# K-transposed-V and query products of an attention and experts kernel, from block-diagonal full-array matmuls to 64-wide tiles

## The chip, the cores and the metric

The kernel runs on one core of a Trainium2 chip. It is one program; its time is the device time from the first to the last instruction in microseconds. A core has engines with queues of their own: TensorE (PE: matmuls, PEld: weight loads), VectorE (DVE), ScalarE (ACT), GpSimd (POOL) and SyncE (SP, which issues most loads here). TensorE reads from SBUF and writes to PSUM, which has 8 banks of 128 partitions by 512 fp32 values.

## The reference

Linear attention without softmax, a norm per head, a layer that takes the maximum of three products, and a layer of eight experts with two experts a token:

```python
kv  = einsum('bhsd,bhse->bhde', k, v)        # 8 batches, 8 heads, 576 tokens, 64 wide
out = einsum('bhsd,bhde->bhse', q, kv)
x   = out / sqrt(mean(out*out, -1) + 1e-6) * g_norm      # then 4608 tokens x 512
h   = maximum(maximum(x @ w1, x @ w2), x @ w3)            # 512 -> 768
x   = h @ w_out                                           # 768 -> 512
logits = x @ w_gate;  noisy = logits + log1p(exp(x @ w_noise)) * noise
# each token: its two best experts e, softmax weight w_e of the two noisy logits
out[token] += w_e * (maximum(x @ e_w1[e], 0) @ e_w2[e])   # 512 -> 1024 -> 512
```

## The kernel before

The 4608 tokens go in 9 chunks of 512, each of four token tiles of 128. The batches of 576 tokens do not line up with the chunks. After the last chunk come the experts, in units of up to 512 tokens; that is the part from about 650 us to the end, and the change does not touch it.

A chunk c has 18 groups of the maximum layer (`g1`, matmuls on line 308), each 12 matmuls: three fp32r passes over the four quarters of the 512 inputs. Its output product (`g2`, line 353) follows in the function `window`, one token tile after the other. Between these stands the attention for the next chunk, written into fixed places of that order by hand:

- in `misc1`, group 10: the K-transposed-V product of batch c + 1 (`kv_pair`, line 188), and `kv_out`, which copies it to SBUF;
- in group 14: the query product (`ao`, lines 209 and 212) of the next chunk's token tiles 0 and 1, and their norms;
- in `window`, between the second and the third token tile: transposes of tiles 0 and 1 (`xtrans`, line 270), the query product of tiles 2 and 3, and their norms; in the middle of the fourth tile's output product the transposes of tiles 2 and 3.

K-transposed-V has one matmul for each pair of heads p (four) and each piece s of 128 tokens (five, the last half filled with zeros). A matmul contracts 128 tokens and gives 128 by 128 values, of which the two 64 by 64 blocks on the diagonal are the two heads. `kv_out` copies these blocks into a buffer KB (`kvbd`) whose other blocks were set to zero at the start. The query product then takes, for each pair of heads, the transposed queries (128 rows: two heads of 64) as weights and KB's 128 by 128 block as the streamed operand. Where a token tile holds tokens of two batches, its halves of 64 tokens are done apart, with 64 weight columns each (line 212). All operands of these two products are fp32; a matmul of them shows in the trace as two weight loads and two matmul records.

A norm (`norm`) is a square on ACT (line 229), a sum per head on DVE (233), a few small steps and the scaling on DVE (249). `xtrans_pe` turns 128 by 128 blocks with TensorE, ACT and DVE then write the high part (line 274) and the low part (279) of x.

Banks come from two rings of four: HB (`hbank`) for the maximum layer, transposes and late query products, AC (`abank`) for the output product, K-transposed-V and early query products. In the start-up (chunk 0 and half of chunk 1) a small planner, `run_tasks`, orders the instructions of all engines by costs and dependences given for each task (`kvp`, `ao`, `n1s`, `t0` and so on); weights arrive as 64-bit numbers there (w1s) and are converted and split by ACT and DVE.

## Time and profile before

| what | value |
|---|---|
| runs | 1589.89 us median of 3 (1589.64 to 1590.69) |
| profiled execution, first to last instruction | 1588.9 us |
| mean granted TensorE clock | 0.997 |
| PE busy | 1564.8 us, 98% of the span |
| DVE, ACT busy | 740.6 us (47%), 608.0 us (38%) |
| chain that ended last | PE 96% |

The profiled execution is shown by its span alone; its time as a run, outside the profile, is not among the three runs of the table. "Busy" sums the times in which an engine had an instruction under way; matmuls overlap, so that the distance between the starts of two stretches says more than a busy time. In a timeline several instructions of one form are merged into a row with their count (xcount); such a row's second number is the time from its first start to its last end, which runs past the next row's start.

### The profile page before, as it was taken

How to read it: one execution, taken by the hardware profiler on the slowest of the kernel's cores; microseconds unless marked ns; L12 is line 12 of the kernel's file. 1: busy time of each engine (PE TensorE's matmuls, PEld its weight loads, DVE VectorE, ACT ScalarE, POOL GpSimd, SP SyncE). 2: the span in 40 equal slices, each digit the busy share in tenths (PEclk: the TensorE clock that was granted, in tenths of full speed). 3: DMA queues.
4: the chain of work that ended last, by engine and by line, in shares of the span. 5: the costliest groups of instructions: out<-in, count | busy, mean ns of one | idle time of the engine just before them, and what ended most of it. 6: DMA issues, size and time to landing. Idle time of an engine off the chain costs nothing.

```text
span 1588.9 us, 21936 instructions
## 1 busy us (share of the span) xinstructions
PE 1564.8 (98%) x8716; PEld 1362.3 (86%) x8716; DVE 740.6 (47%) x1416; ACT 608.0 (38%) x981; POOL 221.6 (14%) x326
## 2 busy tenths in 40 slices
PE   6999999999999999999999999999999999999997
PEld 6899989898989898888888888888888888888886
DVE  6984434343434333445543455455354444544543
ACT  4553323131313132332343445545444343544433
POOL 0001111102020202023211102102111010210102
PEclk9999999999999999999999999999999999999999
DMA  8312732031212101132655567557475554746544
GB/s 305 126 70 106 276 144 113 28 113 47 94 54 87 53 28 54 53 134 107 233 153 146 122 216 218 156 189 205 136 207 154 163 160 155 221 121 203 146 153 75
DMA packets 52572, 219.43 MB, mean 138 GB/s; under 512 B 6896, under 2 KB 7152, under 8 KB 34928
## 3 DMA queue, kind: packets, MB, share of 16 engines
q1 hardware_dynamic: 32608, 166.50, 29.2%
q0 software_dynamic: 19856, 51.48, 14.3%
q8 instruction: 70, 1.15, 0.3%
q14 instruction: 38, 0.31, 0.1%
HBM read 166.49 MB, written 51.47 MB: 137 GB/s over the span
## 4 chain that ended last, share of the span: by engine, by line
PE 96%; DVE 1%; DMA 1%; ACT 1%; issue 1%; POOL 0%; SPq 0%; POOLq 0%; DVEq 0%
PE bank L308 27%; PE bank L1098 25%; PE bank L1036 25%; PE bank L353 10%; PE bank L188 2%; PE bank L760 2%; PE bank L209 2%; PE bank L1050 1%; PE bank L270 1%; DMA G<-w1s 1%; PE bank L493 0%; DMA kv<-kv 0%; PE bank L212 0%; PE bank L485 0%; POOL out L1072 0%
## 5 line engine op out<-in xcount | busy, mean ns | idle before, releaser
L308 PE MATMUL bank<-B,W 128*128 128x512 f32 (+1 forms) x2160 | 454.4, 370 | 6.6 <-ACT W L474 4.9
L308 PEld LDWEIGHTS bank<-B,W 128*128 128x128 f32 x2160 | 375.9, 189 | 75.1 <-ACT W L474 5.6
L1098 PE MATMUL bank<-W,B 128*128 128x512 f32 x1728 | 421.1, 390 | 0.2 <-issue 0.2
L1098 PEld LDWEIGHTS bank<-W,B 128*128 128x128 f32 x1728 | 320.2, 188 | 63.4
L1036 PE MATMUL bank<-B,W 128*128 128x512 f32 (+1 forms) x1728 | 356.9, 344 | 0.0
L1036 PEld LDWEIGHTS bank<-B,W 128*128 128x128 f32 x1728 | 278.0, 189 | 40.1
L290 DVE TENSOR_TENSOR W<-G,W 128x1024 fp32r<-128x1024 f32 x200 | 242.5, 1224 | 132.1 <-ACT W L289 131.5
L1040 ACT ACTIVATE B<-bank 128x512 fp32r<-128x512 f32 (+1 forms) x176 | 91.3, 520 | 373.5 <-PE bank L1036 360.2
L1041 DVE SCALAR_TENSOR_TENSOR B<-bank,B 128x512 fp32r<-128x512 f32 (+1 forms) x176 | 104.3, 593 | 270.8 <-ACT B L1040 265.1
L289 ACT ACTIVATE W<-G 128x1024 fp32r<-128x1024 f32 x200 | 207.7, 1054 | 46.8 <-PE bank L1098 39.3
L353 PE MATMUL bank<-W,B 128*128 128x256 f32 (+1 forms) x1296 | 164.2, 285 | 0.0
L353 PEld LDWEIGHTS bank<-W,B 128*128 128x128 f32 x1296 | 160.2, 188 | 0.7 <-issue 0.2
L419 POOL DMA_INDIRECT Xg<-RA,si x72 | 71.6, 994 | 546.7 <-issue 294.2
L326 DVE TENSOR_TENSOR hm<-hm,bank 128x512 f32<-128x512 f32 (+1 forms) x106 | 69.5, 656 | 138.0 <-PE bank L308 122.8
L1036 PE MATMUL bank<-xlo,W 128*128 128x512 f32 x384 | 102.8, 389 | 0.0
L1072 POOL DMA_INDIRECT out<-xn,idt x37 | 61.2, 1653 | 281.3 <-ACT xn L1103 274.3
L312 ACT ACTIVATE B<-hm 128x512 fp32r<-128x512 f32 (+1 forms) x53 | 32.2, 607 | 173.2 <-DVE hm L326 167.5
L1036 PEld LDWEIGHTS bank<-xlo,W 128*128 128x128 f32 x384 | 72.1, 188 | 15.3
L1072 POOL DMA_INDIRECT out<-x2T,idt x19 | 30.9, 1628 | 272.1 <-ACT x2T L1103 269.7
L764 ACT ACTIVATE B<-bank 128x512 fp32r<-128x512 f32 x76 | 41.5, 596 | 42.3 <-PE bank L760 37.0
L358 ACT ACTIVATE RA<-bank 128x256 f32<-128x256 f32 x72 | 26.3, 384 | 76.6 <-PE bank L353 71.8
L324 ACT ACTIVATE hm<-bank 128x512 f32<-128x512 f32 (+1 forms) x53 | 30.4, 574 | 59.3 <-PE bank L308 47.0
(191 smaller groups left out, 1032.5 us busy)
## 6 DMA issues: line engine op xcount, KB each, us to landing
G<-mw SPq DMA_DIRECT2D x100, 1024.0 KB, 4.8
RB<-Xg SPq DMA_DIRECT2D x13, 1028.0 KB, 7.1
G<-w1s SPq DMA_DIRECT2D x12, 1024.0 KB, 6.4
out<-pad POOLq DMA_DIRECT2D x1, 9472.0 KB
kv<-kv SPq DMA_DIRECT2D x8, 1024.0 KB
G<-kv SPq DMA_DIRECT2D x8, 1024.0 KB, 16.6
RB<-qT SPq DMA_DIRECT2D x8, 1024.0 KB, 5.5
RA<-Xg SPq DMA_DIRECT2D x8, 514.0 KB
```

The source lines that it names most:

```text
L289: ACT.activation(w[:, 0:1024], src, AF.Copy)
L290: DVE.tensor_tensor(w[:, 1024:2048], src, w[:, 0:1024].bitcast(F), op=OP.subtract)
L308: PE.matmul(bank[:, 0:t1 - t0], w_in(g)[:, a, k, s], x[b][:, k, t0:t1], start=n == 0 and k == 0, stop=n == 2 and k == 3)
L326: DVE.tensor_tensor(hm, hm, bank, op=OP.max)
L353: PE.matmul(x2b[i][z][:, 0:hi - lo], h[:, a, s], w[:, b, lo:hi], start=f == 0 and n == 0, stop=f == 5 and n == 2)
L419: i = POOL.indirect_dma_start(out=Xg, out_offset=bass.IndirectOffsetOnAxis(ap=idx, axis=0), in_=src, in_offset=None)
L764: ACT.activation(x[0][:, :, s], t, AF.Copy)
L1036: PE.matmul(bank[:, 0:n], w[:, a, k, s], x[b][:, k, 0:n], start=z == 0, stop=z == 11)
L1040: ACT.activation(h[:, 0, 0:n], bank[:, 0:n], AF.Relu)
L1041: DVE.scalar_tensor_tensor(h[:, 1, 0:n], bank[:, 0:n], 0.0, h[:, 0, 0:n].bitcast(F), op0=OP.max, op1=OP.subtract)
L1072: d = POOL.indirect_dma_start(out=A["out"], out_offset=bass.IndirectOffsetOnAxis(ap=idt[u % 3][:, i:i + 1], axis=0), in_=y, in_offset=None ...
L1098: PE.matmul(obank[i], h[:, a, s], w[:, b, ff % 2, :], start=ff == 0 and n == 0, stop=ff == 7 and n == 2)
```

## The change

Each head gets matmuls of its own, on tiles of the array that are 64 wide.

- K-transposed-V: for each pair and piece two matmuls (h = 0, 1), each with the 64 columns of one head's K as weights and that head's 64 columns of V streamed. The result of head h stands in partitions 64h to 64h + 63, and a batch takes 256 columns of a bank instead of 512. `kv_out` is one copy by DVE, and KB (`kvt`) is 128 by 256 without zero blocks, so its memsets go.
- Query product: `ao` now does two token tiles at once. For each tile, pair, half x of 64 tokens and head h there is one matmul: rows of head h, output partitions of half x. Each row half h writes a bank of its own. So a bank now holds one head of each pair, for both token tiles; the norms work on banks, and the transposes of a token tile read both banks' results. The rows of the first weights are put in the order that this gives, on the host.
- The planner's tasks: one task for a pair of token tiles, and other costs. Transposes wait for both norms.

```diff
-    KB = [sb1.tile([128, 4, 128], F, name=f"kvbd{i}") for i in range(2)]
+    KB = [sb1.tile([128, 256], F, name=f"kvt{i}") for i in range(2)]
...
-    DVE.memset(KB[0], 0.0)
-    POOL.memset(KB[1], 0.0)
+    HALF = [slice(0, 64), slice(64, 128)]
...
             k, v = r[s // 2][2 * (s % 2):2 * (s % 2) + 2]
         else:
             k, v = r[2]
-        PE.matmul(out, k[:, p * 128:(p + 1) * 128], v[:, p * 128:(p + 1) * 128], start=s == 0, stop=s == 4)
+        for h in range(2):
+            o = p * 128 + h * 64
+            PE.matmul(out[HALF[h], :], k[:, o:o + 64], v[:, o:o + 64], start=s == 0, stop=s == 4)
     def kv_pair(b, p, bank):
         for s in range(5):
-            kv_mm(b, p, s, bank[:, p * 128:(p + 1) * 128])
+            kv_mm(b, p, s, bank[:, p * 64:(p + 1) * 64])
     def kv_out(b, bank):
-        v = bank.rearrange("p (a e) -> p a e", a=4)
+        DVE.tensor_copy(KB[b % 2], bank[:, 0:256])
+
+    ao_bank = {}
+
+    def ao(c, j, banks):
         for h in range(2):
-            s = slice(h * 64, h * 64 + 64)
-            (ACT.copy if h else DVE.tensor_copy)(KB[b % 2][s, :, s], v[s, :, s])
-
-    ao_bank = {}
-
-    def ao(c, i, bank):
-        ao_bank[c, i] = bank
-        t0 = c * CT + i * 128
-        b0, b1 = t0 // S, (t0 + 127) // S
-        for p in range(4):
-            o = bank[:, p * 128:(p + 1) * 128]
-            if b0 == b1:
-                PE.matmul(o, qv(c)[:, p, i * 128:(i + 1) * 128], KB[b0 % 2][:, p, :], start=True, stop=True)
-            else:
-                for h, b in ((0, b0), (1, b1)):
-                    PE.matmul(o[h * 64:h * 64 + 64], qv(c)[:, p, i * 128 + h * 64:i * 128 + h * 64 + 64],
-                              KB[b % 2][:, p, :], start=True, stop=True)
+            ao_bank[c, 2 * j + h] = banks[h]
+        for i in range(2):
+            t0 = (2 * j + i) * 128
+            for p in range(4):
+                o = slice(i * 256 + p * 64, i * 256 + (p + 1) * 64)
+                for x in range(2):
+                    t = t0 + x * 64
+                    kb = KB[(c * CT + t) // S % 2]
+                    for h in range(2):
+                        PE.matmul(banks[h][HALF[x], o], qv(c)[HALF[h], p, t:t + 64],
+                                  kb[HALF[h], p * 64:(p + 1) * 64], start=True, stop=True)
     xn_of = {}
     xn_n = [0]
...
     xA = [B2[:, x * 1024:x * 1024 + 1024].rearrange("p (k t) -> p k t", k=4) for x in range(2)]
     def xtrans_pe(c, i, TR=None):
-        x = xn_of[c, i]
         TR = hbank() if TR is None else TR
         for k in range(4):
-            PE.transpose(TR[:, k * 128:(k + 1) * 128], x[:, k * 128:(k + 1) * 128], ident)
+            x = xn_of[c, 2 * (i // 2) + k // 2]
+            o = (i % 2) * 256 + (k % 2) * 128
+            PE.transpose(TR[:, k * 128:(k + 1) * 128], x[:, o:o + 128], ident)
         return TR
     def xtrans_hi(i, t, xT=xT):
...
-            kv_mm(0, p, s, AC[p][:, 0:128])
+            kv_mm(0, p, s, AC[p][:, 0:64])
...
-        for h in range(2):
-            s = slice(h * 64, h * 64 + 64)
-            (ACT.copy if h else DVE.tensor_copy)(KB[0][s, p, s], AC[p][s, s])
+        (ACT.copy if p % 2 else DVE.tensor_copy)(KB[0][:, p * 64:(p + 1) * 64], AC[p][:, 0:64])
...
-    for i in range(4):
-        ao(0, i, abank())
-        norm_a(0, i)
+    for j in range(2):
+        ao(0, j, [abank(), abank()])
+        for i in range(2):
+            norm_a(0, 2 * j + i)
...
-        task(f"t0{i}", "PE", 0.44, [f"n0c{i}"] + ([f"t0{i - 1}"] if i else []), t0, 0,
+        task(f"t0{i}", "PE", 0.44, [f"n0c{i | 1}"] + ([f"t0{i - 1}"] if i else []), t0, 0,
...
-        task(f"kvp{p}", "PE", 1.15, ["kv1"] + ([f"kvp{p - 1}"] if p else []), lambda p=p: kv1(p), 1,
+        task(f"kvp{p}", "PE", 0.6, ["kv1"] + ([f"kvp{p - 1}"] if p else []), lambda p=p: kv1(p), 1,
...
-        task(f"ao{i}", "PE", 0.92, ["q1", "kvo", "x0l3"] + (["ao0"] if i else []), lambda i=i: ao(1, i, abank()), 0)
-        task(f"n1s{i}", "ACT", 0.6, [f"ao{i}", f"t0{i + 2}"], lambda i=i: norm_sq(1, i, x1[i]), 0.6)
+        if i == 0:
+            task("ao0", "PE", 1.0, ["q1", "kvo", "x0l3"], lambda: ao(1, 0, [abank(), abank()]), 0)
+        task(f"n1s{i}", "ACT", 0.6, ["ao0", "t03"], lambda i=i: norm_sq(1, i, x1[i]), 0.6)
...
-        task(f"x1t{i}", "PE", 0.44, [f"n1c{i}"], t1, 0, on_ring(f"x1l{i}"))
+        task(f"x1t{i}", "PE", 0.44, ["n1c0", "n1c1"], t1, 0, on_ring(f"x1l{i}"))
...
-    for i in (2, 3):
-        task(f"ao{i}", "PE", 0.92, ["rest11", f"ao{i - 1}"], lambda i=i: (ao(1, i, hbank()), norm(1, i, RB[:, i * 512 - 1024:i * 512 - 512])),
-             3.5, on_ring(f"ao{i}"))
+    def ao_late():
+        ao(1, 1, [hbank(), hbank()])
+        for i in range(2):
+            norm(1, 2 + i, RB[:, i * 512:i * 512 + 512])
+    task("ao1", "PE", 1.0, ["rest11", "ao0"], ao_late, 3.5, on_ring("ao1", 2))
...
-            for i in range(2):
-                ao(c + 1, i, abank())
+            ao(c + 1, 0, [abank(), abank()])
...
-            if nx and i < 2:
-                ao(c + 1, i + 2, hbank())
+            if nx:
+                if i == 0:
+                    ao(c + 1, 1, [hbank(), hbank()])
...
-    w = np.stack([moe_w1, moe_w2, moe_w3], 0).reshape(3, 4, 128, 6, 128)
+    w = np.stack([moe_w1, moe_w2, moe_w3], 0).reshape(3, 4, 2, 64, DF).transpose(0, 2, 1, 3, 4).reshape(3, 4, 128, 6, 128)
```

In the places below the names are of SBUF and PSUM buffers (kv, G: staged K and V; kvbd, kvt: K-transposed-V; RB: queries; xn: normed x; W: split weights; hm: the running maximum); a last number of a name tells the allocations apart.

TensorE in chunk 2, group 10, two small matmuls of the routing (on trib and onesb) and then the first pair of heads of batch 3, before:

```order
L405 MATMUL bank0_105<-Cb_129,onesb_104 128x40
L406 LDWEIGHTS trib_103
L406 MATMUL bank0_105<-Mb_128,trib_103 128x32
L188 MATMUL bank4_109<-kv0_92 128x128 x2
L188 MATMUL bank4_109<-G1_83 128x128 x2
L188 MATMUL bank4_109<-G2_84 128x128
```

and with the change:

```order
L406 MATMUL bank0_105<-Cb_127,onesb_104 128x40
L407 LDWEIGHTS trib_103
L407 MATMUL bank0_105<-Mb_126,trib_103 128x32
L190 MATMUL bank4_109<-kv0_92 64x64 x4
L190 MATMUL bank4_109<-G1_83 64x64 x4
L190 MATMUL bank4_109<-G2_84 64x64 x2
```

Each matmul of 128 by 128 has become two of 64 by 64; the order of the pairs and pieces is the same, and nothing is moved past them.

TensorE in `window` of chunk 2, the transposes of token tiles 0 and 1 and the query product of tiles 2 and 3, before:

```order
L353 MATMUL bank6_111<-W11_81,B2_87 128x272
L270 MATMUL bank1_106<-cst_98,xn0_93 128x128 x4
L270 MATMUL bank2_107<-cst_98,xn1_94 128x128 x4
L209 MATMUL bank3_108<-kvbd1_91,RB_89 128x128 x4
L209 MATMUL bank0_105<-kvbd1_91,RB_89 128x128 x4
L353 MATMUL bank7_112<-W9_79,B1_86 128x256
```

and with the change, the first two of the query product's 32 matmuls:

```order
L271 MATMUL bank1_106<-cst_98,xn0_93 128x128 x2
L271 MATMUL bank1_106<-cst_98,xn1_94 128x128 x2
L271 MATMUL bank2_107<-cst_98,xn0_93 128x128 x2
L271 MATMUL bank2_107<-cst_98,xn1_94 128x128 x2
L212 MATMUL bank3_108<-kvt1_91,RB_89 64x64
L212 MATMUL bank0_105<-kvt1_91,RB_89 64x64
```

The two transposes of each result bank now read two normed tiles, and the matmuls of the query product alternate between two banks, one a head.

DVE in the start-up, from the last step of one conversion (ISA, G1) to the low part of the second weight tile (W1), before:

```order
L457 ISA G1_83<-G1_83,RB_89 128x1024x2
L448 TENSOR_SCALAR RB_89<-G2_84 128x1024
L449 SCALAR_TENSOR_TENSOR RB_89<-G2_84,RB_89 128x1024
L470 SCALAR_TENSOR_TENSOR RA_88<-G1_83 128x1024
L326 TENSOR_TENSOR hm0_96<-hm0_96,bank6_111 128x512
L233 TENSOR_REDUCE stat_121<-xn2_95 128x8
L233 TENSOR_REDUCE stat_121<-x2T0_97 128x8
L237 TENSOR_SCALAR stat_121<-stat_121 128x16
L478 TENSOR_TENSOR W1_71<-RA_88,W1_71 128x1024
```

and with the change:

```order
L458 ISA G1_83<-G1_83,RB_89 128x1024x2
L471 SCALAR_TENSOR_TENSOR RA_88<-G1_83 128x1024
L233 TENSOR_REDUCE stat_119<-xn2_95 128x8
L233 TENSOR_REDUCE stat_119<-x2T0_97 128x8
L479 TENSOR_TENSOR W1_71<-RA_88,W1_71 128x1024
L327 TENSOR_TENSOR hm0_96<-hm0_96,bank6_111 128x512
L237 TENSOR_SCALAR stat_119<-stat_119 128x16
L449 TENSOR_SCALAR RB_89<-G2_84 128x1024
L450 SCALAR_TENSOR_TENSOR RB_89<-G2_84,RB_89 128x1024
```

The planner has put the first steps of the third conversion (on G2) and a maximum (hm) behind the low part of the second weight tile.

## Rows read from the trace of the kernel before

**Rows 1.** the page: busy time, chain by engine, largest matmul group

```profile
PE 1564.8 (98%) x8716; PEld 1362.3 (86%) x8716; DVE 740.6 (47%) x1416; ACT 608.0 (38%) x981; POOL 221.6 (14%) x326
...
PE 96%; DVE 1%; DMA 1%; ACT 1%; issue 1%; POOL 0%; SPq 0%; POOLq 0%; DVEq 0%
...
L308 PE MATMUL bank<-B,W 128*128 128x512 f32 (+1 forms) x2160 | 454.4, 370 | 6.6 <-ACT W L474 4.9
```

**Rows 2.** TensorE's timeline in chunk 3: start us, us, line, op, xcount

```profile
298.99 0.69 PE L188 MATMUL bank<-kv 128*128 128x128 f32 x4
299.52 0.83 PE L188 MATMUL bank<-G 128*128 128x128 f32 x6
...
302.87 0.83 PE L188 MATMUL bank<-G 128*128 128x128 f32 x6
303.46 11.18 PE L308 MATMUL bank<-B,W 128*128 128x512 f32 x48
314.47 1.95 PE L209 MATMUL bank<-kvbd,RB 128*128 128x128 f32 x16
316.18 11.14 PE L308 MATMUL bank<-B,W 128*128 128x512 f32 x48
...
336.81 1.95 PE L209 MATMUL bank<-kvbd,RB 128*128 128x128 f32 x16
338.52 6.84 PE L353 MATMUL bank<-W,B 128*128 128x256 f32 x54
345.19 0.60 PE L270 MATMUL bank<-cst,xn 128*128 128x128 f32 x4
```

**Rows 3.** TensorE's timeline in chunk 2, query product of tiles 0 and 1

```profile
237.53 1.06 PE L209 MATMUL bank<-kvbd,RB 128*128 128x128 f32 x8
238.51 1.09 PE L212 MATMUL bank<-kvbd,RB 128*64 128x128 f32 x16
239.54 11.19 PE L308 MATMUL bank<-B,W 128*128 128x512 f32 x48
```

**Rows 4.** short stretches, line L212 alone: records in flight (x), clock, DMA

```profile
238.50:238.55 0.05, 0.04 (x2) 0.04 (x2) 1.00 0.00 0
238.55:238.66 0.11, 0.11 (x2) 0.11 (x4) 1.00 0.00 0
238.66:238.70 0.04, 0.04 (x4) 0.04 (x4) 1.00 0.00 0
238.70:238.77 0.07, 0.07 (x4) 0.07 (x4) 1.00 0.00 0
238.77:238.80 0.03, 0.03 (x6) 0.03 (x4) 1.00 0.00 0
```

**Rows 5.** TensorE's timeline: matmuls of 16 streamed columns, and what follows them

```profile
102.96 1.86 PE L493 MATMUL bank<-wgn,G 128*128 128x16 f32 x16
104.66 3.11 PE L308 MATMUL bank<-B,W 128*128 128x256 f32 x24
```

**Rows 6.** timelines of ACT and DVE in chunk 3: first square, last scaling

```profile
337.90 0.60 ACT L229 ACTIVATE xn<-bank 128x512 f32<-128x512 f32 x1
...
343.42 0.69 DVE L249 TENSOR_TENSOR x2T<-bank,stat 128x512 f32<-128x512 f32 x1
```

**Rows 7.** the timelines of TensorE and DVE at the end of chunk 1

```profile
173.61 8.96 PE L353 MATMUL bank<-W,B 128*128 128x256 f32 x72
...
177.27 0.43 DVE L316 TENSOR_TENSOR B<-hm,B 128x256 fp32r<-128x256 f32 x1 [0.49 <-ACT B L312]
```

**Rows 8.** the chain that ended last: start us, us, what

```profile
5.66 6.44 PE bank L188 x34
...
13.43 8.07 DMA G<-w1s
...
28.06 5.37 PE bank L308 x16
```

**Rows 9.** SP's waits up to 60 us: total us, times, longest us

```profile
SPq L511 <- PE bank L188: 3.8, 1, 3.8
```


## Prediction

> **What bounds the kernel now.** I read the page's chain first, then TensorE's row there, then TensorE's timeline chunk by chunk, last the DVE and ACT timelines around it. The reader is to see in the chain that TensorE holds 96% of it, and in the page's group that the largest matmul line waited 6.6 us in the whole run, 4.9 of that for one ACT line in the start-up [rows 1]. After the start-up, from about 47 us on, TensorE hardly waits, so an edit that gives it fewer or more nanoseconds moves the end by as much; before that, loads, DVE and ACT set the pace. One chunk of the steady part [rows 2] has three stretches that the change rewrites: the K-transposed-V product of the next batch, 40 records from 298.99 to 303.46 us (4.47 us, 112 ns a record), the query product of its first two token tiles, 16 records from 314.47 to 316.18 (1.71 us), and that of the last two, 336.81 to 338.52 (1.71 us). An fp32 matmul leaves two such records, each a weight load and a stream, so 20 matmuls are 40 records.
>
> **The change part by part.** All counts are of records of the steady part and the second half of the start-up.
>
> K-transposed-V: 40 records become 80, each with 64 weight columns and 64 streamed columns on one of two column halves. Six batches (2 to 7) lie where TensorE sets the end; batches 0 and 1 lie in the start-up.
>
> Query product: 16 records for two token tiles become 64, each 64 by 64 on one of four quarters (two row halves by two column halves). There are 18 such pairs of token tiles; two are in chunk 0 in the start-up, 16 count. In 4 of the 16 a token tile holds two batches and runs on column halves already: there 8 full records and 16 half ones took 237.53 to 239.54, 2.01 us [rows 3].
>
> These half records are the nearest rows to the new form, and the sum hangs on them. Each streams 128 columns through a half with 64 weight columns. In [rows 4] two of them begin within the first 0.05 us, none in the next 0.11, two more by 238.70, none in 0.07, two more by 238.80: two records every 0.11 us. So both halves work at once, and each takes some 110 ns for 128 streamed columns, as the full array does (112). Streaming half as many should halve that; weight loading does not hinder it, since 128 weight columns with only 16 streamed ones pace at 1.70 us for 16 records, 106 ns [rows 5], so 64 need about 53. I take 112/2 = 56 ns a record on one tile: 28 ns a record with two tiles at work, 14 with four.
>
> Going into and out of the halves costs something: 2.01 us less 8 records at 107 ns (1.71/16) and 16 at 55 leaves 0.28 us, which I charge to every tiled stretch, and which the four mixed ones pay already.
>
> With r the ns per tiled record, a K-transposed-V stretch becomes 0.28 + 0.080 r, a query stretch 0.28 + 0.064 r. Gains: 6 x (4.47 - 0.28 - 0.080 r) + 12 x (1.71 - 0.28 - 0.064 r) + 4 x (2.01 - 0.28 - 0.064 r) = 49.2 - 1.504 r us. It crosses zero at r = 33. Bounds of r: 14 for the query product if all four tiles overlap; 55, what the half-array records average, if halving the columns saves nothing because records cannot come faster than in the one row that shows them, or 56 if tiles don't overlap. I take 28 for K-transposed-V and 14 for the query product, the measured pace scaled by columns and by tiles: 6 x 1.95 + 12 x 0.53 + 4 x 0.83 = 11.7 + 6.4 + 3.3 = 21.4 us.
>
> The waits that move: a norm now needs a whole pair of token tiles, and the transposes of either tile need both norms. In the last-two stretch the first square began 1.09 us after the product (337.90, when ACT was free from its other work) and the second norm ended at 344.11 (343.42 + 0.69), 1.08 us before the transposes at 345.19 [rows 2, 6]. With a 1.18 us product (0.28 + 0.90) the first square starts some 0.2 later, the norms end at about 344.3, and TensorE reaches the transposes 0.53 earlier, at 344.66: 0.36 us of cover is left, cost nothing; were it gone, each 0.1 us would cost 0.1 us in each of seven chunks. Queued behind these transposes stand the last 18 records of the output product L353, and behind them the next chunk.
> Chunk 1 has no cover: its groups stream 256 columns, DVE runs the norms before the last split, which lies at 177.27 to 177.70, and TensorE wants its result 34 records of 8.96/72 = 0.124 us after 173.61, at 177.8 [rows 7]. DVE would be 0.3 later and TensorE 0.5 earlier: 0.8 us lost, once (0 to 1).
>
> The start-up. SP's second load of K and V waited 3.8 us for TensorE to read the first, the first weights of the maximum layer (w1s) are queued behind it, and their landing at 21.50 starts the chain that ends with the first wide matmul at 28.06 [rows 8, 9]. The first product took 6.44 us there; with smaller records it follows the loads closely, and what SP issues behind it comes up to 2 us earlier, of which the DMA engines, busy already, pass on part. The planner also puts the second weight split earlier on DVE. Against this stands that TensorE idles longer before 28 us. I take 0.5 us gained, between 1.5 lost and 3 gained. The removed ACT copies and memsets of the block-diagonal buffers lie beside TensorE's work: nothing.
>
> Sum: 21.4 - 0.8 + 0.5 = 21.1 us. The profiled execution spans 1588.9 us; the median of the runs, 1589.89, is 1.0 above that, which I leave as it is: 1588.9 + 1.0 - 21.1 = 1568.8, say 1569 us.
>
> **Rivals.**
> Row halves do not overlap, or matmuls start in the order of the program, so that the two records of one tile hold up the next tile: r is 28 in both products, 49.2 - 42.1 = 7.1, less 0.8, plus 0.5: 1583 us. For it: no row of before splits the rows, and on average two tiles cannot be told from strict order by pace alone. Against: in strict order the first record of the run would start alone, and [rows 4] shows two in the first 0.05 us.
> The Trainium skill, "TensorE: Matmul & The Clock Gate", Part 3 on packing small matmuls, has matmuls start and end in strict program order, only weight loads being pulled ahead; by it the time would be this rival's, and [rows 4] speaks against it.
>
> Records cannot be supplied faster: TensorE is given four times as many instructions for the query product, and the densest row of before holds 55 ns a record over 16 records only. If a longer run can do no better than that pace, r = 55, 49.2 - 82.7 = -33.5, less 0.3: about 1624 us, slower. It decides from r = 33 on. The same price falls due if tiles do not overlap at all, the change then not doing what it says. For it: nothing in the trace shows a longer run under 107 ns a record. Against: four records and four weight loads begin within 0.2 us in [rows 4], and no wait for supply shows.
> The Trainium skill, "TensorE: Matmul & The Clock Gate", Part 1 on the clock gate, gives about 62 ns of sequencer work a matmul where the hardware does not decode it; by it r would be 62 and the time about 1634. The 55 ns average of the half records is under that, but over 16 records only.
>
> Supply at a middle pace, r 33 to 50 for the query product alone: 1588 to 1605 us.
>
> The norms lose their cover: 0.36 us short of need in seven chunks would be 2.5 us, 1571; it lies within the forecast's own range.
>
> **How the numbers follow.** Four tiles overlap as forecast: 0.53, 1562 to 1576. Half the overlap: 0.21, 1577 to 1587. Middle pace, or no difference: 0.11. Supply-bound or no overlap: 0.15. The measurement tells about 0.2%, 3.2 us, from no change: faster takes the first two cases and none of the others, 0.74; same 0.07; slower 0.19. The range of 8 in 10 is 1561 to 1602: the low end has the start-up gaining 3 and the entry cost vanishing in part; the high end leaves out the last case alone.
>
> **What would show it.** Query stretches of the new profile at about 1.2 us with four matmul starts inside some 0.06 us, and K-transposed-V at about 2.5 us, confirm the first case; 2.1 us for the query stretch with pairs of starts is the second; 3.8 us is the third. Transposes that wait for a DVE norm in each window show the lost cover, and a gap before the output product near 177 us the 0.8. The first wide matmul before 28 us shows the start-up term. A forecast off by more than the start-up's bounds with these stretches right would mean that something after 47 us that I take as untouched has moved.

## The result, and the profile after

The changed kernel takes 1573.41 us (median of 4 runs, 1572.87 to 1574.52), the kernel before beside it 1589.77 (1589.45 to 1590.69): a ratio of 0.9897, 95% interval 0.9883 to 0.9911. That is 16.4 us gained where 21 were forecast, inside the range, 4 us above the predicted 1569.

The page of the kernel after, to be read against [rows 1]: busy time of TensorE, the chain by engine, the largest matmul group.

```profile
PE 1543.8 (98%) x9868; PEld 1337.2 (85%) x9868; DVE 740.1 (47%) x1413; ACT 604.5 (38%) x972; POOL 221.3 (14%) x325
...
PE 97%; DMA 1%; DVE 1%; ACT 1%; issue 0%; POOL 0%; SPq 0%; POOLq 0%; DVEq 0%
...
L309 PE MATMUL bank<-B,W 128*128 128x512 f32 (+1 forms) x2160 | 455.7, 371 | 6.6 <-ACT W L475 4.2
```

TensorE has 1152 more records (9868 for 8716) and is busy 21 us less. It still holds nearly the whole chain, and the largest group waits the same 6.6 us as before.

TensorE's timeline in chunk 3, to be read against [rows 2]: start us, us, line, xcount.

```profile
295.91 0.45 PE L190 MATMUL bank<-kv 128*64 128x64 f32 x8
...
297.94 0.52 PE L190 MATMUL bank<-G 128*64 128x64 f32 x12
298.39 11.17 PE L309 MATMUL bank<-B,W 128*128 128x512 f32 x48
309.50 1.16 PE L212 MATMUL bank<-kvt,RB 64*64 64x64 f32 x64
310.59 11.18 PE L309 MATMUL bank<-B,W 128*128 128x512 f32 x48
...
331.36 1.16 PE L212 MATMUL bank<-kvt,RB 64*64 64x64 f32 x64
332.45 6.86 PE L354 MATMUL bank<-W,B 128*128 128x256 f32 x54
339.15 0.38 PE L271 MATMUL bank<-cst,xn 128*128 128x128 f32 x2
```

From start to start the 80 records of the K-transposed-V product take 2.48 us (295.91 to 298.39) where 40 took 4.47, and the 64 of a query product 1.09 (309.50 to 310.59, 331.36 to 332.45) where 16 took 1.71.

The records of the first query stretch inside the first 0.15 us, from the view of short windows, line L212 alone (stretch, its length, PE busy, PEld busy, with the records in flight behind x, then the granted clock and the DMA share and rate):

```profile
309.49:309.52 0.03, 0.02 (x4) 0.02 (x4) 1.00 0.00 0
309.52:309.56 0.04, 0.04 (x4) 0.04 (x5) 1.00 0.00 0
...
309.62:309.64 0.03, 0.03 (x8) 0.03 (x12) 1.00 0.00 0
```

Four matmuls are under way at 309.52, none joins them in the next 0.04 us: the four starts lie 6 to 7 ns apart. By the starts in the trace, from the second group on the groups follow each other every 58.5 ns, 14.6 ns a record. All four tiles work at once.

Where does the difference of the two traces grow? The output product (L353 before, L354 after) starts in chunk 0 at 120.97 before and 123.97 after, in the last chunk at 699.89 and 683.60, by these rows of before

```profile
120.97 0.73 PE L353 MATMUL bank<-W,B 128*128 128x256 f32 x4
...
699.89 0.52 PE L353 MATMUL bank<-W,B 128*128 128x256 f32 x3
```

and these of after:

```profile
123.97 0.75 PE L354 MATMUL bank<-W,B 128*128 128x256 f32 x4
...
683.60 0.64 PE L354 MATMUL bank<-W,B 128*128 128x256 f32 x4
```

So the kernel after is 3.0 us late at the end of the start-up, gains 19.3 us from there to the last chunk, and is 16.3 us ahead. A second profile of the kernel before, `before_again` below, has the first of these points at 122.11 and the same 578.92 us from there to the last chunk: the gain of the steady part is firm, the loss of the start-up is 1.9 or 3.0 by the execution that it is held against. (The two profiled spans, 1588.9 and 1571.0, differ by 17.9; the 1.6 between is the delay in the profile of before that the run `before_again` deals with below. It lies in the experts, which begin at 719 us before and 703 after, not near 650.)

The start-up after, where the 3 us are; rows of before are in [rows 8, 9]. First TensorE's timeline:

```profile
20.56 0.48 PE L190 MATMUL bank<-pad,hm 128*64 128x64 f32 x4 [0.73 <-DMA pad<-kvr]
...
22.93 0.67 PE L190 MATMUL bank<-kv 128*64 128x64 f32 x8
...
24.17 1.56 PE L271 MATMUL bank<-cst,xn 128*128 128x128 f32 x10
...
30.59 5.53 PE L309 MATMUL bank<-B,W 128*128 128x512 f32 x16 [4.20 <-ACT W L475]
```

And ACT's there:

```profile
22.64 1.18 ACT L445 ACTIVATE G<-G 128x1024 int32<-128x1024 uint32 x1 [4.11 <-DMA G<-w1s]
25.11 1.84 ACT L275 ACTIVATE B<-bank,gn 128x512 fp32r<-128x512 f32 x3 [1.29 <-PE bank L271]
26.84 1.11 ACT L454 ACTIVATE G<-G 128x1024 f32<-128x1024 f32 x1
```

The same steps in the kernel before (the piece, the transposes, the first weights):

```profile
19.27 0.46 PE L188 MATMUL bank<-pad,hm 128*128 128x128 f32 x2 [0.37 <-DMA pad<-kvr]
...
20.68 1.47 PE L270 MATMUL bank<-cst,xn 128*128 128x128 f32 x12
...
21.52 1.19 ACT L444 ACTIVATE G<-G 128x1024 int32<-128x1024 uint32 x1 [2.95 <-DMA G<-w1s]
```

TensorE waits until 20.56 for the last piece of batch 1's K and V (`pad<-kvr`, used at 19.27 before), runs all four pairs, and reaches the transposes of x only at 24.17 (20.68 before). On ACT the first weights were ready at 22.64 (21.52 before), but its next step on them (L454, 26.84) stands behind three evacuations of those transposes (L275, 25.11). The first wide matmul starts at 30.59 instead of 28.06.

### The profile page after: what moved, and what is told of

Its sections match the earlier page's. It is cut to its first block, busy times and chain, and to the rows that moved or that the text cites. A ratio compares the mean times of both kernels' runs of the same rounds, so it can differ in the third digit from the quotient of the medians.

```text
span 1571.0 us, 24229 instructions
## 1 busy us (share of the span) xinstructions
PE 1543.8 (98%) x9868; PEld 1337.2 (85%) x9868; DVE 740.1 (47%) x1413; ACT 604.5 (38%) x972; POOL 221.3 (14%) x325
## 3 DMA queue, kind: packets, MB, share of 16 engines
q8 instruction: 79, 1.29, 0.3%
## 4 chain that ended last, share of the span: by engine, by line
PE 97%; DMA 1%; DVE 1%; ACT 1%; issue 0%; POOL 0%; SPq 0%; POOLq 0%; DVEq 0%
PE bank L309 28%; PE bank L1102 26%; PE bank L1040 25%; PE bank L354 10%; PE bank L764 2%; PE bank L190 1%; PE bank L212 1%; PE bank L1054 1%; PE bank L271 1%; DMA pad<-kvr 1%; DMA G<-kv 0%; PE bank L494 0%; ACT B L275 0%; PE bank L486 0%; POOL out L1076 0%
## 5 line engine op out<-in xcount | busy, mean ns | idle before, releaser
L1102 PEld LDWEIGHTS bank<-W,B 128*128 128x128 f32 x1728 | 320.2, 188 | 63.4
L354 PE MATMUL bank<-W,B 128*128 128x256 f32 (+1 forms) x1296 | 164.3, 285 | 0.0
L354 PEld LDWEIGHTS bank<-W,B 128*128 128x128 f32 x1296 | 160.1, 188 | 1.1
L1076 POOL DMA_INDIRECT out<-hm,idt x19 | 32.8, 1727 | 145.1 <-ACT hm L1107 141.3
```

The costliest lines, as they stand in the source:

```text
L354: PE.matmul(x2b[i][z][:, 0:hi - lo], h[:, a, s], w[:, b, lo:hi], start=f == 0 and n == 0, stop=f == 5 and n == 2)
L1076: d = POOL.indirect_dma_start(out=A["out"], out_offset=bass.IndirectOffsetOnAxis(ap=idt[u % 3][:, i:i + 1], axis=0), in_=y, in_offset=None ...
L1102: PE.matmul(obank[i], h[:, a, s], w[:, b, ff % 2, :], start=ff == 0 and n == 0, stop=ff == 7 and n == 2)
```

## The experiments

The start-up can be undone without touching the rest, so most runs split it from the steady part. Times are medians; a ratio is against the kernel before on the same chip.

**s_full: the start-up back on the full array.** Batches 0 and 1 and chunks 0 and 1 get the full-array products, block-diagonal buffers KD beside KB, and one norm a token tile; GpSimd copies batch 1's result to KB later.

```diff
+    def kv_tiled(b):
+        return False if b < 2 else True
+    def ao_tiled(c):
+        return False if c < 2 else True
     def kv_mm(b, p, s, out):
+        if not kv_tiled(b):
+            PE.matmul(out, k[:, p * 128:(p + 1) * 128], v[:, p * 128:(p + 1) * 128], start=s == 0, stop=s == 4)
+            return
...
-        task(f"t0{i}", "PE", 0.44, [f"n0c{i | 1}"] + ([f"t0{i - 1}"] if i else []), t0, 0,
+        task(f"t0{i}", "PE", 0.44, [f"n0c{i}"] + ([f"t0{i - 1}"] if i else []), t0, 0,
-        task(f"kvp{p}", "PE", 0.6, ["kv1"] + ...
+        task(f"kvp{p}", "PE", 1.15, ["kv1"] + ...
```

> Start-up as before (batches 0 and 1 and the query products of chunks 0 and 1 as full-array matmuls, planner's tasks as before), small tiles from batch 2 and chunk 2 on. Both theories: the first wide matmul at 28.1 us, the output product of chunk 0 at 121 us instead of 123.97, time about 1570.4 (1573.4 less 3.0). A theory that the start-up's lateness is made up later anyway says 1573. Under theory A the clock reaches its full level near 10.7 us as in the kernel before.

Measured: 1570.05 us (1569.89 to 1570.91), ratio 0.9875 (0.9860 to 0.9890). TensorE's start-up there:

```profile
19.09 0.46 PE L198 MATMUL bank<-pad,hm 128*128 128x128 f32 x2 [0.53 <-DMA pad<-kvr]
...
20.57 1.87 PE L318 MATMUL bank<-cst,xn 128*128 128x128 f32 x12
...
28.43 5.52 PE L356 MATMUL bank<-B,W 128*128 128x512 f32 x16 [3.16 <-ACT W L522]
```

The piece is used at 19.09, the transposes start at 20.57, the first wide matmul at 28.43, chunk 0's output product at 121.46: the start-up is the old one but for half a microsecond, as was expected. From there to the last chunk (681.25) it takes 559.79 us; the kernel after takes 559.63, the one before 578.92. So the loss lies in the start-up alone, and this kernel is the fastest of the study, ahead of the kernel before beyond doubt, and of the changed one by 3 us, with intervals that still touch (0.9883 to 0.9890).

**s_full_kv and s_full_ao: one product at a time.** As s_full, with only the K-transposed-V product of batches 2 to 7, or only the query product of chunks 2 to 8, on tiles.

```diff
 s_full_kv, against s_full:
     def ao_tiled(c):
-        return False if c < 2 else True
+        return False if c < 2 else False
 s_full_ao, against s_full:
     def kv_tiled(b):
-        return False if b < 2 else True
+        return False if b < 2 else False
```

> Start-up on the full array as in the kernel that took 1570.05 us; after it only the K-transposed-V product of batches 2 to 7 is on tiles, every query product is a full-array one. If the two products' gains are separate and add up, the time is 1570.05 + 11 x 0.52 + 3 x 0.85 = 1578.3 us (1577 to 1579.5), the K-transposed-V stretches 2.5 us and the query stretches 1.7. If the query product's gain exists only beside the other (norms that are late without it), another time.

> As the last, but only the query products of chunks 2 to 8 are on tiles, the K-transposed-V product of batches 2 to 7 on the full array. Separate gains: 1570.05 + 6 x 1.85 = 1581.2 us (1580 to 1582.5), query stretches 1.1 us, K-transposed-V stretches 4.5. The gain of 1.7 us in the first experts, which the trace of the changed kernel shows beside that of the kernel before, was foreseen by nobody: if it hangs on tiles at all, it should be present in one of these two kernels and not in the other; if the trace of before caught a single delay there, both have it (about 853.5 us from the first expert matmul to the last one's start).

Measured: 1578.72 us (1577.78 to 1580.32), ratio 0.9921 (0.9904 to 0.9937), and 1581.93 (1581.65 to 1583.08), ratio 0.9945 (0.9928 to 0.9961). From chunk 0's output product to the last chunk's they take 567.61 and 571.06 us. Against s_full's 559.79 the query product is worth 7.8 us in 14 stretches, the K-transposed-V product 11.3 in 6; their sum, 19.1, is what before loses against s_full on that way (19.13). The gains are separate and add up, and both times lie in the expected ranges. From the first to the last of the 168 expert products (start to start) both take 853.5 us, so that part hangs on neither.

**ao_order: the same matmuls, four on one tile in a row.**

```diff
-            for p in range(4):
-                o = slice(i * 256 + p * 64, i * 256 + (p + 1) * 64)
-                for x in range(2):
-                    t = t0 + x * 64
-                    kb = KB[(c * CT + t) // S % 2]
-                    for h in range(2):
+            for x in range(2):
+                t = t0 + x * 64
+                kb = KB[(c * CT + t) // S % 2]
+                for h in range(2):
+                    for p in range(4):
+                        o = slice(i * 256 + p * 64, i * 256 + (p + 1) * 64)
```

> The changed kernel with the loops of the query product turned: four matmuls in a row on the same tile before the next tile's, instead of going round the four tiles. If each tile takes its matmuls independently of the order of the program: the query product stays at 1.1 us for 64 records, time 1573 to 1575. If matmuls start strictly in the order of the program: 64 records at 58 ns, 3.7 us instead of 1.09, 16 times 2.6 us more, about 1615. In between (a short reach ahead): 1.3 to 2.5 us for 64 records, 1577 to 1595.

Measured: 1595.26 us, one run, slower than the kernel before beside it (1589.72). A query stretch of chunk 3 and what follows it, from TensorE's timeline:

```profile
317.17 2.69 PE L212 MATMUL bank<-kvt,RB 64*64 64x64 f32 x64
319.79 11.17 PE L309 MATMUL bank<-B,W 128*128 128x512 f32 x48
```

The stretch takes 2.62 us, 2.4 times the 1.09; this and the time lie just beyond the in-between case. One tile alone paces its records 52 to 59 ns apart. From about the fifth of a tile's eight records on, some starts lie 4 to 6 ns behind another, which I read as the next tile's. So a matmul behind others of another tile can start, but only a few records ahead: the overlap of four needs neighbours in the program that lie on different tiles. The order of the loops is worth 22 us, more than the whole change.

**warm: is the start-up slow by TensorE's clock?** 60 full-array bf16 matmuls on a tile of ones, into a bank that is free, before the first product and after the first query product.

```diff
+    def warm(n):
+        for _ in range(n):
+            PE.matmul(HB[0][:, 0:128], ones, ones, start=True, stop=True)
+    warm(40)
...
+    warm(20)
```

> The changed kernel with 40 full-array bf16 matmuls of ones ahead of the first product, while TensorE waits for the loads, and 20 more behind the query product of chunk 0. Nothing reads them. Theory A: the clock is at its full level when the first product starts, its records go at 29 ns each instead of 53, the first wide matmul comes 1.5 to 2.5 us earlier than 30.59 and the time is 1570.5 to 1572. Rival B: the small products get faster but the first wide matmul stays within 0.7 us of 30.59, time 1572.5 to 1574.

Measured: 1573.06 us (1571.52 to 1574.00), ratio 0.9892 (0.9877 to 0.9907), the same as without. Granted clock by stretch (third number from the end of a row):

```profile
8.50:11.90 3.40, 2.79 (x48) 2.60 (x48) 0.45 (x2) 0.42 (x2) 0.00 (x0) 0.50 0.99 374
...
18.70:25.50 6.80, 5.37 (x77) 5.09 (x78) 4.74 (x7) 1.19 (x1) 0.00 (x0) 0.50 0.82 293
```

The added matmuls gave the upper level (2.4 GHz) from 5.1 us on, but it fell to the lower one (0.50) at 8.5 and again at 18.7, just where batch 1's pairs run, and the first wide matmul came at 31.02. So the run doesn't tell the clock's price; its time is that of rival B.

**kvcost: is it the planner's cost?** One number, the cost that the planner has for a pair of the K-transposed-V product, is what it was before.

```diff
-        task(f"kvp{p}", "PE", 0.6, ["kv1"] + ...
+        task(f"kvp{p}", "PE", 1.15, ["kv1"] + ...
```

> The changed kernel with one number put back: the planner's cost of a K-transposed-V task is 1.15 again instead of 0.6, so that the transposes of x stand between the pairs of batch 1 as in the kernel before. Theory A (TensorE's clock stays at the lower level through the start-up because the small matmuls leave it waiting): the clock history is as in the changed kernel, the first wide matmul at 30 to 30.6 us, time 1572.5 to 1574. Rival B (the planner's order costs the start-up: all of batch 1's product ahead of the transposes): the first wide matmul comes at about 28.5 us and the time is 1570.5 to 1571.5.

Measured: 1578.33 us (1575.38 to 1579.73), ratio 0.9925 (0.9912 to 0.9939): 5 us above the changed kernel, which neither theory had. The planner now sets transposes between the pairs (22.54 instead of 24.17), and the first wide matmul gains 0.4 us (30.20), as theory A said. But the last pair moves behind them, and the next rows show who waits for it. SP's queue:

```profile
26.72 0.33 SPq L171 DMA_DIRECT2D kv<-qT  x1
```

ACT, the third weights:

```profile
34.20 1.19 ACT L445 ACTIVATE G<-G 128x1024 int32<-128x1024 uint32 x1 [4.06 <-DMA G<-w1s]
```

TensorE, the waits for these:

```profile
41.15 7.33 PE L309 MATMUL bank<-B,W 128*128 128x512 f32 x24 [2.27 <-ACT W L475]
...
51.71 8.54 PE L309 MATMUL bank<-B,W 128*128 128x512 f32 x35 [1.86 <-ACT W L475]
```

The load of chunk 1's queries (L171) goes into the buffer that the pairs read, so it leaves at 26.72 instead of 23.63, the third weights behind it on SP's queue; ACT has them at 34.20 instead of 31.02, and TensorE waits 2.27 and 1.86 us for weights that it had in time before. Each time the granted clock then falls to 0.50 for 3.4 us (41.6 to 45.0 and 51.9 to 55.3; in the kernel after once, from 48.6 on), so that the waits cost more than their length. The pairs are the head of one chain and the transposes of another; moving either in front costs at the other.

**s_kvfull and s_aofull: which product upsets the start-up?** s_kvfull: the K-transposed-V product of batches 0 and 1 on the full array, all query products on tiles, planner's cost 1.15. s_aofull: the reverse, planner's cost 0.6.

```diff
 s_kvfull, against s_full:
     def ao_tiled(c):
-        return False if c < 2 else True
+        return True if c < 2 else True
 s_aofull, against s_full:
     def kv_tiled(b):
-        return False if b < 2 else True
+        return True if b < 2 else True
-        task(f"kvp{p}", "PE", 1.15, ["kv1"] + ...
+        task(f"kvp{p}", "PE", 0.6, ["kv1"] + ...
```

> The K-transposed-V products of batches 0 and 1, in the start-up, are full-array matmuls again (their two diagonal blocks copied out); all query products stay on tiles, the first chunks' too. In the changed kernel the first wide matmul starts at 30.59 us instead of 28.06, and chunk 0's output product at 123.97 instead of 120.97; with both products of the start-up on the full array these are 28.43 and 121.46, and the run takes 1570.05 us. Theory A (the quicker K-transposed-V product lets the second load of K and V out earlier, its pieces and the first weights share the DMA engines and land later, and the transposes stand behind all four pairs): this kernel has the first wide matmul at 28 to 29 us, chunk 0's output product at about 121, and takes 1569 to 1570.5 us. Theory B (the query product on tiles is what is late, since a transpose now needs the norms of two token tiles): the first wide matmul stays at about 30.5 and the time at about 1573.

> The other half: the query products of chunks 0 and 1 are full-array matmuls with a norm for each token tile, the K-transposed-V products of batches 0 and 1 stay on tiles. Theory A: the first wide matmul stays at about 30.5 us and the time at 1573 to 1574.5 (two query stretches lose 0.5 to 0.8 us each, one of them where TensorE waits anyway). Theory B: 28 to 29 us and about 1570.

Measured: 1578.11 us (1576.27 to 1579.26), ratio 0.9915 (0.9899 to 0.9932), with the first wide matmul at 31.43; and 1573.60 (1572.15 to 1574.60), ratio 0.9893 (0.9876 to 0.9909), with it at 30.19. Theory A holds for s_aofull and fails for s_kvfull. Theory B fails for s_aofull and is right for s_kvfull on the late start only, the time being 5 us above what it said. Either product on tiles is enough for a late start. In s_kvfull the planner, with transposes that need two norms, puts the third pair between them, and the chain of kvcost repeats (waits of 2.25 and 1.87 us). On the clock s_aofull tells something, by its row of a long stretch:

```profile
16.20:29.70 13.50, 6.53 (x110) 5.79 (x109) 10.89 (x18) 7.90 (x13) 0.00 (x0) 1.00 0.82 302
```

and TensorE's timeline in that stretch:

```profile
20.92 0.34 PE L202 MATMUL bank<-pad,hm 128*64 128x64 f32 x4 [1.08 <-DMA pad<-kvr]
...
21.64 0.43 PE L202 MATMUL bank<-kv 128*64 128x64 f32 x8
...
22.35 1.53 PE L318 MATMUL bank<-cst,xn 128*128 128x128 f32 x12
...
30.19 5.32 PE L356 MATMUL bank<-B,W 128*128 128x512 f32 x16 [5.14 <-ACT W L522]
```

ACT there, the evacuations and the first weights:

```profile
23.04 2.42 ACT L322 ACTIVATE B<-bank,gn 128x512 fp32r<-128x512 f32 x4 [3.18 <-PE bank L318]
25.34 1.12 ACT L492 ACTIVATE G<-G 128x1024 int32<-128x1024 uint32 x1
```

The clock is at its upper level from 16.2 to 29.7, eight K-transposed-V records take 0.43 us (0.67 at 22.93 in the kernel after), the transposes start at 22.35, and still the first wide matmul comes at 30.19. So the slow pace of the small matmuls is real, and without it the start is late all the same. But s_aofull does not give the price of that pace in the kernel after, because it is late in another way: its planner sets all four evacuations ahead of the first weights on ACT, which takes these at 25.34, though DVE already works on them at 23.04.

**hold_w1: do the earlier loads hinder each other?** The second weights leave only after DVE's second sum. The run also adds a small buffer (scr).

```diff
     load_w1(0)
-    load_w1(1)
...
             norm_a(0, 2 * j + i)
+        if j == 0:
+            scr = st("scr", [128, 1])
+            DVE.memset(scr, 0.0)
+            SP.dma_start(scr, A["gn"])
+            load_w1(1)
```

> The changed kernel with one load held back: SP issues the second weight tile of the maximum layer (w1s, 1024 KB) only after DVE has reduced the squares of the second token tile (near 16.1 us instead of 12.7; a transfer of 512 bytes that waits for a DVE memset stands ahead of it). Nothing else is moved. Theory A (transfers that are let out earlier share the DMA engines, so that the last piece of K and V and the first weights land later): the last piece lands well before 20.56, by 19.0 us or earlier, the first weights before 22.0, the transposes start near 22 instead of 24.17, the first wide matmul at 28 to 29 instead of 30.59, and the run takes 1570 to 1571.5 us. Theory C (the start-up's loss lies in TensorE's lower granted clock and its small matmuls alone): the first wide matmul stays between 30 and 31 and the time at 1573.

Measured: 1589.87 us (1586.17 to 1590.27, 10 runs), ratio 0.9988 (0.9979 to 0.9997); the load is held as meant, and nothing of theory A happens; the first wide matmul is where theory C has it, the time is not. SP's queue:

```profile
16.62 0.62 SPq L438 DMA_DIRECT2D G<-w1s  x1
```

TensorE:

```profile
21.00 0.48 PE L190 MATMUL bank<-pad,hm 128*64 128x64 f32 x4 [1.02 <-DMA pad<-kvr]
...
30.45 5.51 PE L309 MATMUL bank<-B,W 128*128 128x512 f32 x16 [4.16 <-ACT W L475]
```

The piece is used at 21.00, later still, the first wide matmul starts at 30.45. So holding the second weights does not let the piece land sooner. The span is 17.1 us longer than the changed kernel's. Of this, 1.4 us lie ahead of chunk 0's output product, 8.1 in chunk 1 and 7.9 in the experts. In chunk 1 the K-transposed-V tiles take 2.0 us more and a query stretch 3.8 more, both with TensorE standing still "for issue" (waiting for nothing that the profile shows), and the 48 records behind them 2.4 more, with the granted clock at 0.50 from 174.1 to 181.0. In the experts 2.0 us go at one place near 741 us, again with waits for issue, and 5.8 accrue evenly: part of the wide matmuls start every 234 ns instead of 227. Why that is so stays open, and with the added buffer the run changes more than one load. The next runs are about the waits for issue.

**best and best_again: two steps more.** s_full with chunk 1's second query product on tiles (GpSimd copies batch 1's result earlier for that), and in chunks 3 to 6 the K-transposed-V product moved from group 10 to group 14, right ahead of the query product.

```diff
-    def ao_tiled(c):
-        return False if c < 2 else True
+    def ao_tiled(c, j=1):
+        return c > 1 or (c == 1 and j == 1)
...
-        if 0 < c < NB - 1 and g == 10:
+        if 0 < c < NB - 1 and g == (10 if c < 3 else 14):
             bank = abank()
             for p in range(4):
                 kv_pair(c + 1, p, bank)
             kv_out(c + 1, bank)
```

> The kernel with the full-array start-up (1570.05 us) and two steps more: chunk 1's second query product, near 120 us, is on tiles too (0.7 us less, from the 1.79 to 1.09 us of that stretch), and in chunks 3 to 6 the K-transposed-V product stands right ahead of the next query product, so that one entry into the tiles and one exit serve both (four times, some 0.3 us each by the records at the borders of a stretch, 1.2 us). 1568.2 us if both count; 1569.4 if entry and exit cost nothing of their own; about 1570 or more if a norm or a load comes late by the move.

> The kernel with the full-array start-up, chunk 1's second query product on tiles and the joined stretches of chunks 3 to 6, a second time and unchanged. At its first run it took 1603.74 us: in chunks 1 and 3 to 6 TensorE stood still inside its tiled stretches, some 0.6 us after every five records, always while GpSimd's indirect scatter was writing; the kernel with one load held back showed the same in chunk 1 and with the first experts. Theory P (it belongs to the program: a tiled stretch that meets the scatter in time is starved): the same stalls in the same places and 1601 to 1605 us. Theory E (it belonged to the chip at that hour: the changed kernel and six others also run the K-transposed-V tiles of chunk 1 during the scatter, and show no such stall): no waits for issue in the tiled stretches, and 1568 to 1570 us.

Measured: 1603.74 us (1601.78 to 1605.11), ratio 1.0077 (1.0063 to 1.0090), and on another chip 1603.01 (1602.15 to 1604.56), ratio 1.0073 (1.0057 to 1.0090): slower than before, both times. No case of the first expectation had that; of the second it is theory P. Against the trace of s_full chunk 1 costs 8.1 us more and chunks 3 to 6 cost 5.6 to 6.8 more each. The joined stretch of chunk 3 on TensorE:

```profile
312.22 0.45 PE L202 MATMUL bank<-kv 128*64 128x64 f32 x8
...
314.70 0.80 PE L258 MATMUL bank<-kvt,RB 64*64 64x64 f32 x18
315.88 0.36 PE L258 MATMUL bank<-kvt,RB 64*64 64x64 f32 x6 [0.37 <-issue]
...
319.51 0.69 PE L258 MATMUL bank<-kvt,RB 64*64 64x64 f32 x27 [1.10 <-issue]
320.13 12.76 PE L356 MATMUL bank<-B,W 128*128 128x512 f32 x48
```

GpSimd in it, an issue of the scatter:

```profile
315.14 0.97 POOL L467 DMA_INDIRECT Xg<-RA,si  x1 [0.22 <-issue]
```

TensorE's waits for issue at the query product in the whole run (us in total, times, longest):

```profile
PE bank L258 <- issue: 10.6, 22, 1.1
```

and in the second run:

```profile
PE bank L258 <- issue: 10.1, 24, 1.1
```

The K-transposed-V part runs as ever (2.48 us). From 315.3 on, as the scatter's data moves, TensorE does some five records and starts no other for 0.6 us, again and again, until the stretch ends at 320.13. The next 48 records take 12.76 us instead of 11.18, with the granted clock at 0.50 from 320.2 to 323.6. The joining thus moved the tiles into the time of the scatter: in the kernel after, chunk 3's stretches (295.91 to 298.39, 309.50 to 310.59) end before the scatter's transfers begin (299 and 312). What it saves at the borders can't be read from this run. That meeting the scatter is not all of it, chunk 1 shows: there the K-transposed-V tiles run beside the scatter for 2.3 us in all kernels that have them, without a stall in eight, and with 2 us of stalls in hold_w1 and best. What in these two programs differs stays open. That TensorE's instructions arrive late, an obvious candidate, is not shown: of the instruction loads (queue q8 of the page, 16 KB each) one moves at 313.6 and the next at 321.2, both outside the stall of chunk 3.

**before_again: the kernel before, profiled once more.**

> The kernel before, unchanged, profiled a second time. In its first profile the last 168 expert products take 855.17 us from the first to the last one's start, with a delay of 1.7 us near 747 us in which ACT and DVE begin nothing; in the profiles of all nine kernels with tiles they take 853.5. If that delay belongs to one execution, this profile shows 853.5 and a span near 1587.5 us; if it belongs to the kernel before, it shows 855.2 again.

Measured: 1590.44 us, span 1588.7, not the 1587.5 expected, because the start-up is 1.1 us longer here (chunk 0's output product at 122.11). The first to the last expert product take 853.87 us here, 855.17 in the first profile, 853.48 after. The first profile's delay, on DVE:

```profile
745.48 0.69 DVE L1041 SCALAR_TENSOR_TENSOR B<-bank,B 128x512 fp32r<-128x512 f32 x1 [4.71 <-issue]
```

DVE stood still for 4.71 us "for issue" beside a scatter; the second profile has no such wait. It belonged to one execution and is no gain of the change. (At the same place, in the first experts, hold_w1 loses 2.0 us and best 1.8.)

## Why the prediction was right or wrong

**The two products: right.** Pace and overlap were as forecast: 29.3 ns a record against 28 for K-transposed-V, 14.6 against 14 for the query product, stretches of 2.48 and 1.09 us against 2.5 and 1.18. What each is worth in a chunk is read from output product to output product against the kernel before: in s_full_ao a pair of query stretches gains 0.99 us (0.50 each; 0.53 forecast), in s_full_kv K-transposed-V gains 1.90 (1.95 forecast). The charge for going into and out of the tiles was right: 1.71 less 0.50 less 64 records at 14.6 ns leaves 0.28 us, 4.47 less 1.90 less 80 at 29.3 leaves 0.23, against 0.28 taken. From chunk 0's output product on, 21.4 less the two query stretches ahead of it (0.83 + 0.53) and the 0.8 make 19.2; measured 19.3. That these are so close is in part luck: the 0.8 was not lost, K-transposed-V gave 0.4 less than forecast (11.3 for 11.7) and the query product 0.5 less (7.8 for 8.3).

**The rivals: refuted by the runs.** Strict order would have needed r = 28 in the query product; four starts within 20 ns and 14.6 ns show the opposite. ao_order shows in what sense order does count: the chip looks only a few records ahead, and with four matmuls of one tile in a row r is 36 and the change loses. The Trainium skill, "TensorE: Matmul & The Clock Gate", Part 3, has matmuls of different tiles run at once, each starting some 4 ns after the last, and has them start and end in strict program order. The trace agrees with the first (6 to 7 ns), and ao_order disagrees with the second: strict order would have made its stretch 3.7 us, 2.62 were measured. The supply bound did not show in this kernel, whose 64 records in 0.94 us are far under r = 33. By Part 1 of the same page of the Trainium skill r would have been 62 if the hardware did not decode the matmuls; the trace doesn't agree with that case. But best and hold_w1 show that tiles can be held back by far more: with the scatter beside them, they fell to five records in 0.73 us, r = 146, and the span of best is 33 us longer than that of s_full. Whether that is a bound of supply is open.

**The start-up: wrong, and the step that moved the sum.** I took 0.5 gained with bounds of 1.5 lost and 3 gained. At chunk 0's output product the kernel is 3.0 behind (1.9 behind before_again), though two query stretches of the sum (1.36 forecast) lie ahead of that point: 4.9 us off (3.7), outside the bounds either way. The time stayed inside the range because its upper end was set by the rivals, not because such a start-up was foreseen. The step that failed is "with smaller records it follows the loads closely, and what SP issues behind it comes up to 2 us earlier". SP did issue 1.3 us earlier (the first weights at 12.15 for 13.43), and they arrived 1.1 later. The table shows, for the last piece of K and V, its issue and its use, and how many packets (8 KB each) of the weights queued behind it had ended when its last packet did:

| kernel | K product / query product in the start-up | piece issued | piece used | weight packets ahead of it | first weights used | first wide matmul |
|---|---|---|---|---|---|---|
| s_full | full / full | 13.22 | 19.09 | 3 | 21.80 | 28.43 |
| before | full / full | 12.79 | 19.27 | 0 | 21.52 | 28.06 |
| best_again | full / full | 12.56 | 19.30 | 0 | 21.50 | 28.04 |
| best | full / full | 12.32 | 19.55 | 0 | 21.69 | 28.58 |
| before_again | full / full | 12.26 | 19.92 | 5 | 22.11 | 29.06 |
| s_full_kv | full / full | 12.03 | 19.31 | 3 | 21.68 | 28.48 |
| s_kvfull | full / tiles | 11.97 | 20.22 | 44 | 22.29 | 31.43 |
| s_full_ao | full / full | 11.84 | 20.06 | 4 | 22.22 | 28.83 |
| ao_order | tiles / tiles | 11.70 | 20.54 | 31 | 22.61 | 31.00 |
| kvcost | tiles / tiles | 11.67 | 21.06 | 59 | 23.12 | 30.20 |
| after | tiles / tiles | 11.51 | 20.56 | 40 | 22.64 | 30.59 |
| hold_w1 | tiles / tiles | 11.46 | 21.00 | 62 | 23.18 | 30.45 |
| warm | tiles / tiles | 11.38 | 20.83 | 70 | 22.91 | 31.02 |
| s_aofull | tiles / full | 11.16 | 20.92 | 62 | 23.04 | 30.19 |

By and large, the earlier it leaves, the later it is used. This holds even among the seven full / full rows, which run the same instructions in the same order there (best and best_again with two copies on GpSimd more), so that their spread is that of single executions. The DMA engines are busy throughout in all of them (a share of 1.0 from 8 to 18 us, 364 to 382 GB/s), and up to 20 us they move 6.70 MB after and 6.74 before, so an earlier issue could bring nothing. What it costs shows in the packets: with the old start-up 0 to 5 packets of the weights queued behind the piece get ahead of it, with either product on tiles 31 to 70. Why they do is open, and whether holding the first weights would help was not run; hold_w1 held only the second.

The late landing is only 1.1 of the 2.5 us to the first wide matmul. In the full / full rows this comes 6.5 to 7.0 us after the first weights, in the kernel after 7.95. The 1.0 to 1.4 us more are the transposes, for which ACT waits 1.29 us (its row at 25.11): the planner sets all four pairs, and so the late piece, ahead of them, and a pair takes 1.07 us there, 0.59 in s_aofull at the upper clock. How much is the order and how much the pace, no run separates; ACT evacuates the transposes before it goes on with the weights in both kernels. I had read in the order on DVE that the second split comes earlier, and not that the transposes on TensorE now stand behind two pairs more.

From the first wide matmul to chunk 0's output product the kernel after takes 93.4 us and the one before 92.9, although two query stretches there are shorter (1.36 forecast). TensorE's clock at its lower level from 48.6 to 52.0 us (0.50 in the row below; in the kernel before it is 1.00 there) may hold 1.7 of that, an estimate: half of 3.4 us. At the first wide matmul both kernels have such a stretch (31.6 to 34.9 after, 27.7 to 31.1 before).

```profile
48.60:52.00 3.40, 3.36 (x17) 3.06 (x16) 3.32 (x4) 1.40 (x3) 0.00 (x0) 0.50 0.15 31
```

That it fell there after waits of 0.65, 0.16 and 0.92 us from 45.7 on is what the trace shows; no run took these waits away alone. In ao_order, where the clock stays up from 33.9 us on, the same way takes 94.6 us with two query stretches of 1.53 us more each, so 91.5 without them, which fits.

**Chunk 1's 0.8: not lost.** From chunk 0's output product to chunk 1's the kernel gains 2.41 us (50.23 for 52.64), the 1.90 and 0.50 of one K-transposed-V and one query stretch. The output product there (174.20 on) has no gap although DVE's last split ends at 178.77, 37 records after its start; it is wanted later than the 34 records that I counted. The norms of the steady chunks kept their cover: 0.49 us are left ahead of the transposes at 339.15 (0.36 forecast).

**The span and the median.** The profiled execution of before held 1.6 us of delay that is not the kernel's, and a run's time lies 1.7 to 1.9 above its span in the runs seen here, not 1.0. The two errors partly cancel.

## What to carry to other kernels

Small independent matmuls on quarters of the array run four at a time if neighbours in the program lie on different tiles; multiply records by the pace of one tile (58 ns here) over four, and add about a quarter of a microsecond a stretch. Treat a start-up that waits for loads as a part by itself: freeing a buffer sooner brought nothing here while the DMA engines were full, and a planner with new costs can put the wrong work in front, so try the change with the old start-up, and profile a start-up twice: with the same instructions it differed by 1.1 us. Dense stretches of small matmuls are safer clear of an indirect scatter in time (two of the eleven programs with such tiles lost 10 us and more beside it): look there for waits "for issue" before joining or moving them.

## What the runs showed of the hardware

Unexpected was that TensorE can stand still for issue in a tiled stretch while an indirect scatter writes: five records, then 0.6 us of nothing, 10.6 us of waits in the run of best, the same on two chips. And that program order counts over a reach of a few records: 64 identical matmuls took 1.09 or 2.62 us by their order alone.
